# The first MoE's way in by seven block products for two of its three pairs of feature tiles, and one list scheduler for the order of both MoEs

## The chip, the core and the metric

The kernel runs on one core of one Trainium2 chip. Five engines work beside each other, each through its own instructions in order: TensorE (PE) multiplies matrices into PSUM, VectorE (DVE), ScalarE (ACT) and GpSimd (POOL) work on elements, SyncE (SP) issues most DMA transfers. The metric is the device time of one execution, in microseconds (us); lower is better.

## The reference, cut to what matters

```python
mask   = q_bucket[:, :, :, None] == k_bucket[:, :, None, :]      # buckets from 6 sign bits of q @ proj, k @ proj
scores = where(mask, q @ k.T / sqrt(64), -1e9)                   # batch 2, 8 heads, 768 tokens, 64 features
x = softmax(scores) @ v                                          # laid out as 1536 tokens x 512 features
h = maximum(maximum(x @ w1, x @ w2), x @ w3)                     # first MoE: 512 -> 768 ...
x = h @ w_out                                                    # ... -> 512
h = x @ w_in                                                     # second MoE: 512 -> 2048
g = h * (1 / (1 + exp(-1.702 * h)))
out = g @ w_out2                                                 # -> 512
```

The weights are 64-bit floats in memory, everything else is 32-bit.

## The kernel before, in words

Every float32 product is made of three TensorE products: each operand is split into a high part, rounded to the format TensorE takes (`xh`, `whi`), and the low rest (`xl`, `wlo`), and high x high, low x high and high x low are added up in one PSUM bank. A split costs one ACT cast and one subtraction. A matmul of the MoEs multiplies a 128x128 block of weights with 512 tokens; the 1536 tokens make three chunks.

**Attention** fills the first part of the time. Its order is written by a planner (`plan`, with the costs of `COST` and the due times of `DUE`). Its last tasks prepare the first four weight blocks of the first MoE, load two more, and compute chunk 0 of the first feature tile.

**First MoE, way in** (`up1`, L606): six feature tiles of 128, three weight matrices, three chunks: 54 units of 12 matmuls, of which attention's planner issues three. ACT copies a unit of `w1` out of PSUM (L614), DVE takes the maximum with those of `w2` and `w3` (L616), ACT and POOL split the result (L626, L627). **Way out** (`down1`, L639): 12 units of 18 matmuls, split into `xh`, `xl` of the second MoE (L643, L644).

**Second MoE**: eight groups of two feature tiles. The way in of group 0 is dense (`up2`, L667). In groups 1 to 7 the two tiles, with chunks 0 and 1, form a 2x2 block product, which `seven` computes by seven block products of six matmuls in place of eight (L793), from four sums of weight blocks (S1 to S4, made on POOL, L527 to L534, split at L539 and L544) and four sums of tokens (T1 to T4, made once). Chunk 2 stays dense, in half units of six matmuls. P1, P6, P7 and P4 add to one bank one behind another, and ACT copies the bank out between them (L753); P5 and P3 share another, which DVE adds to an earlier copy in between (L749). Then the gelu (L680 to L685), and the **way out** (`down2`, L817), whose result DVE adds to `res` (L822).

**Weight blocks.** A block (128x512, 512 KB as 64-bit words) is loaded into one of two `wraw` buffers (L436) and turned into float32: absolute value on ACT (L450), clamp on POOL (L454), a shift and two bit operations on DVE (L462, L466, L470), then the split, a cast on ACT (L477) and a subtraction on POOL (L497). 58 blocks go through this.

**What sets the order of the MoEs**: `unit` issues a PE unit, then the steps that the unit before left in `due`, then the next step of each weight block in flight (`w_tick`, at a rate of one block per `PACE` units in the first MoE). Every choice of an engine is written in the code. `in_order` then holds each engine to the order of the code. PSUM has eight banks of 128x512 for the MoEs, the weight splits four buffers, `hm` three, `hc` four.

Of the kernel before, what the change touches and what calls it, by code (L numbers as in the profile page):

```python
# [8 lines left out]
U32 = mybir.dt.uint32  # L9
# [80 lines left out]

def build(tc, q, k, v, proj, w1, w2, w3, w_out, m2_in, m2_out, out):
# [23 lines left out]
    shared = ("xh", "xl", "hm0", "wraw", "wbits", "wmag")  # L115
# [292 lines left out]
    for ft in range(FT):  # L408
        for i, w in enumerate((w1, w2, w3)):
            w_block(("up", ft, i), w[:, ft * P:(ft + 1) * P].rearrange("(c p) f -> p c f", p=P), EC, "w")  # L410
    w_out_group(0)
# [6 lines left out]
    for n in range(FT2 // FG):  # L418
        for f in range(n * FG, (n + 1) * FG):
            w_block(("in", f), m2_in[:, f * P:(f + 1) * P].rearrange("(c p) f -> p c f", p=P), EC, "w")  # L420
        if n > 0:
            w_out_group(n)
    WIDE = w1.dtype == U64
    WRAW = 2
    WBUFS = {"w": 4, "wo": 4}
    wraw, wsplit, wf = {}, {}, {}
    wstate = [0, 0]
    wstage = [False]

    def w_load():  # L430
        i = wstate[0]
        if i < len(wblocks):
# [8 lines left out]
            wstate[0] += 1  # L441

    def w_steps(i, fine=False):

        _, n, tag = wblocks[i]
        got = {}

        def magnitude():
            got["m"] = st([P, EC, P], "wbits", 2)[:, :n]
            nc.scalar.activation(got["m"], f32(words()[1]), AF.Abs)  # L450

        def clamp():

            nc.gpsimd.tensor_scalar(out=got["m"], in0=got["m"], scalar1=MOST, scalar2=LEAST, op0=ALU.min, op1=ALU.max)  # L454
# [5 lines left out]
        def shift():  # L460
            got["w"] = st([P, EC, P], "wmag", 4, U32)[:, :n]
            nc.vector.tensor_scalar(out=got["w"], in0=got["m"].bitcast(U32), scalar1=5, scalar2=2, op0=ALU.logical_shift_left,  # L462
                                    op1=ALU.logical_shift_right)

        def low():
            nc.vector.scalar_tensor_tensor(out=got["w"], in0=words()[0], scalar=29, in1=got["w"],  # L466
                                           op0=ALU.logical_shift_right, op1=ALU.bitwise_or)

        def sign():
            nc.vector.scalar_tensor_tensor(out=got["w"], in0=words()[1], scalar=0xC0000000, in1=got["w"],  # L470
                                           op0=ALU.bitwise_and, op1=ALU.bitwise_or)

        def split():
            t = f32(got["w"]) if WIDE else wraw[i][:, :n]
            hi = st([P, EC, P], tag + "hi", WBUFS[tag], F32R, sb if tag == "w" else mo[0])
            lo = st([P, EC, P], tag + "lo", WBUFS[tag], F32R, sb if tag == "w" else mo[0])
            nc.scalar.copy(hi[:, :n], t)  # L477
            got["s"] = (hi, lo, t)
            if not WIDE:
                w_load()  # L480

        def bits():
            shift()
            low()
            sign()
            w_load()

        def whole():
            sign()
            w_load()  # L490
            wf[i] = f32(got["w"])
            if i in wpair:
                wflight.append((None, sum_steps(wpair[i])))

        def lower():
            hi, lo, t = got["s"]
            nc.gpsimd.tensor_tensor(out=lo[:, :n], in0=t, in1=f32(hi[:, :n]), op=ALU.subtract)  # L497
            wsplit[i] = (hi, lo)
        if fine:
            return [magnitude, clamp, shift, low, sign, split, lower]  # L500
        if WIDE and wstage[0]:

            return [magnitude, clamp, None, None, shift, low, whole, None, split, None, lower]
        return ([magnitude, clamp, bits] if WIDE else []) + [split, lower]

    wflight = []

    wpair = {wplace["in", 2 * p + 1]: p for p in range(1, FT2 // 2)}

    def w_free(i):  # L510

        tag = wblocks[i][2]
        mine = [j for j in range(i) if wblocks[j][2] == tag]
        return len(mine) < WBUFS[tag] or mine[-WBUFS[tag]] in wdone

    def sums_free():
        return len(sums) == len(sdone)

    def sum_steps(p):

        a1, a2 = (wf[wplace["in", 2 * p + n]] for n in range(2))
        got = {}

        def first():
            got["x"] = st([P, 2, 2, P], "hm0", 2)
            s1, s2 = (got["x"][:, n] for n in range(2))
            nc.gpsimd.tensor_tensor(out=s1, in0=a2[:, 0:2], in1=a2[:, 2:4], op=ALU.add)  # L527
            nc.gpsimd.tensor_tensor(out=s2, in0=s1, in1=a1[:, 0:2], op=ALU.subtract)

        def second():  # L530
            got["y"] = st([P, 2, 2, P], "hm0", 2)
            s3, s4 = (got["y"][:, n] for n in range(2))
# [20 lines left out]
    def w_tick(start):  # L553

        for entry in list(wflight):
# [4 lines left out]
            if step:  # L560
                step()
# [549 lines left out]
```

## Time and profile before

| what | value |
|---|---|
| median of 3 runs | 695.25 us (694.95 to 695.7) |
| the profiled execution | 695.35 us, span of its trace 693.5 us |
| PE | 687.7 us busy, 99% of the span, 3742 matmuls |
| DVE, ACT, POOL | 73%, 55%, 65% of the span |
| the chain that ended last | PE 92%, DVE 5% |

The span runs from the first to the last instruction of the trace; the execution is 1.85 us longer. The chain that ended last is followed back from the last instruction, at each step to what released it. A share of busy time is a mean over attention and the MoEs, which have different limits.

### The profile page before, as it was taken

Reading aid. Unit: us, or ns where it says so; the run is one execution under the profiler, and the core shown is the slowest. Engines: PE = TensorE matmul, PEld = TensorE weight load, DVE = VectorE, ACT = ScalarE, POOL = GpSimd, SP = SyncE. Lnnn points to the kernel's source line nnn. Section 1 sums busy time; section 2 is a strip of 40 time slices with the busy share of each in tenths; the row PEclk is TensorE's granted clock in tenths of the full one; section 3 lists DMA queues with packets and bytes.
Section 4 is the critical chain, followed back from the end, with each engine's and each line's share of the span. In section 5 each row is a group of like instructions: output and inputs, shape, how many; then the busy total and the mean of one; then the engine's idle time right before and its main releaser. Section 6 shows DMA issues by size and latency. Waiting matters only on the chain.

```text
span 693.5 us, 10887 instructions
## 1 busy us (share of the span) xinstructions
PE 687.7 (99%) x3742; PEld 589.9 (85%) x3742; DVE 503.7 (73%) x888; ACT 379.9 (55%) x745; POOL 452.3 (65%) x492
## 2 busy tenths in 40 slices
PE   9999999999999999999999999999999999999998
PEld 5899999999999988888888888888888888888886
DVE  7999999999999915644554455537878777777855
ACT  4898898888889823323233333565453544444440
POOL 5487878788888845425435432595959678786842
PEclk9999999999999999999999999999999999999999
DMA  5657577778554012322112112013121222212104
GB/s 116 143 126 159 131 176 155 169 170 179 114 125 120 19 39 91 92 64 89 55 60 92 46 53 66 27 60 92 41 81 61 72 67 76 61 60 92 31 0 183
DMA packets 74408, 63.35 MB, mean 91 GB/s; under 512 B 41377, under 2 KB 65185, under 8 KB 74353
## 3 DMA queue, kind: packets, MB, share of 16 engines
q1 hardware_dynamic: 74128, 62.52, 34.7%
q8 instruction: 30, 0.49, 0.3%
q14 instruction: 26, 0.20, 0.1%
q10 hardware_dynamic: 224, 0.13, 0.1%
HBM read 38.80 MB, written 3.15 MB: 60 GB/s over the span
## 4 chain that ended last, share of the span: by engine, by line
PE 92%; DVE 5%; DMA 1%; issue 1%; SPq 0%; ACT 0%; POOL 0%; DVEq 0%; POOLq 0%; ACTq 0%
PE acc L606 20%; PE acc L817 19%; PE acc L793 10%; PE acc L667 8%; PE PV L355 8%; PE S L307 8%; PE T L337 8%; PE acc L639 7%; DVE ptl L347 2%; DVE se L314 2%; PE T L205 2%; PE T L178 1%; PE T L606 1%; DMA raw<-in_v_dram 0%; DMA raw<-in_q_dram 0%
## 5 line engine op out<-in xcount | busy, mean ns | idle before, releaser
L685 POOL TENSOR_TENSOR gl<-hm,gh 128x512 fp32r<-128x512 f32 x48 | 70.1, 1465 | 53.4 <-ACT gh L684 53.4
L328 POOL TENSOR_SCALAR se<-se,rc 128x768 f32<-128x768 f32 x96 | 87.5, 923 | 25.6 <-DVE rc L325 9.1
L347 DVE TENSOR_TENSOR ptl<-T,pth 128x512 fp32r<-128x512 f32 x144 | 94.5, 683 | 4.0 <-ACT pth L343 3.8
L320 ACT ACTIVATE se<-se,mn 128x768 f32<-128x768 f32 x96 | 90.9, 947 | 5.4 <-DVE se L314 4.8
L314 DVE TENSOR_SCALAR_CACHE_REDUCE se<-S 128x768 f32<-128x768 f32 x96 | 91.0, 950 | 1.8 <-PE S L307 1.6
L343 ACT CAST pth<-T 128x512 fp32r<-128x512 f32 x144 | 80.2, 588 | 12.7 <-PE T L337 10.6
L307 PE MATMUL S<-kst,qst 128*128 128x512 f32 (+3 forms) x384 | 87.0, 350 | 0.0
L337 PE MATMUL T<-ident,se 128*128 128x128 f32 x576 | 80.4, 273 | 0.8 <-DVE ptl L347 0.6
L606 PE MATMUL acc<-xh,whi 128*128 128x512 f32 x204 | 79.4, 389 | 0.0
L606 PE MATMUL acc<-xl,whi 128*128 128x512 f32 x204 | 79.4, 389 | 0.0
L606 PE MATMUL acc<-xh,wlo 128*128 128x512 f32 x204 | 79.4, 389 | 0.0
L817 PE MATMUL acc<-wohi,gh 128*128 128x512 f32 (+1 forms) x194 | 75.0, 387 | 0.0
L817 PE MATMUL acc<-wolo,gh 128*128 128x512 f32 (+1 forms) x194 | 75.0, 387 | 0.0
L355 PE MATMUL PV<-pth,vst 128*128 128x256 f32 x288 | 74.4, 293 | 0.0
L462 DVE TENSOR_SCALAR wmag<-wbits 128x512 uint32<-128x512 uint32 (+1 forms) x58 | 43.3, 747 | 38.9 <-POOL wbits L454 38.8
L450 ACT ACTIVATE wbits<-wraw 128x512 f32<-128x512 f32 (+1 forms) x58 | 37.9, 655 | 61.2 <-DMA wraw<-in_moe_w_dram 29.9
L497 POOL TENSOR_TENSOR wlo<-wmag,whi 128x512 fp32r<-128x512 f32 (+1 forms) x42 | 58.9, 1402 | 18.2 <-ACT whi L477 18.2
L337 PEld LDWEIGHTS T<-ident,se 128*128 128x128 f32 x576 | 65.4, 140 | 6.0 <-DVE ptl L347 1.1
L355 PE MATMUL PV<-ptl,vst 128*128 128x256 f32 x288 | 70.2, 279 | 0.0
L616 DVE TENSOR_TENSOR hm<-acc,hm 128x512 f32<-128x512 f32 x34 | 23.5, 690 | 56.8 <-PE acc L606 54.4
L307 PEld LDWEIGHTS S<-kst,qst 76*128 76x128 f32 (+1 forms) x384 | 59.2, 190 | 5.2 <-DVE se L314 0.5
L470 DVE SCALAR_TENSOR_TENSOR wmag<-wraw,wmag 128x512 uint32<-128x512 uint32 (+1 forms) x58 | 61.4, 1058 | 1.4
(163 smaller groups left out, 1604.3 us busy)
## 6 DMA issues: line engine op xcount, KB each, us to landing
wraw<-in_moe_w_dram SPq DMA_DIRECT2D x18, 512.0 KB
wraw<-in_moe_w_out_dram SPq DMA_DIRECT2D x16, 512.0 KB
wraw<-in_moe_w_in_dram SPq DMA_DIRECT2D x16, 512.0 KB
kst<-kq SPq DMA_DIRECT2D x42, 192.0 KB
qst<-kq SPq DMA_DIRECT2D x42, 192.0 KB
raw<-in_k_dram SPq DMA_DIRECT2D x16, 192.0 KB
raw<-in_q_dram SPq DMA_DIRECT2D x16, 192.0 KB
raw<-in_v_dram SPq DMA_DIRECT2D x16, 192.0 KB
```

The lines of the kernel that those rows point to most:

```text
L307: nc.tensor.matmul(pss[:, x], qs[r, k, c * P:(c + 1) * P], ks[r, k, x], start=k == 0, stop=k == 1)
L314: nc.vector.tensor_scalar(out=se[u], in0=pss[:, :S], scalar1=1.0e9, scalar2=None, op0=ALU.min, op1=ALU.min, accum_out=mn[u])
L320: nc.scalar.activation(se[u], se[u], AF.Exp, bias=mn[u], scale=-1.0, accum_out=sm[u // 2][:, u % 2:u % 2 + 1])
L328: nc.gpsimd.tensor_scalar(out=se[u], in0=se[u], scalar1=rc[u // 2][:, u % 2:u % 2 + 1], scalar2=1.0, op0=ALU.mult, op1=ALU.mult)
L337: nc.tensor.transpose(pst[:, i * P:(i + 1) * P], se[2 * jq + o][:, c * P:(c + 1) * P], ident)
L343: nc.scalar.copy(ptr[jq][0][:, n * 512:(n + 1) * 512], tps[jq, n])
L347: nc.vector.tensor_tensor(out=ptr[jq][1][:, s], in0=tps[jq, n], in1=f32(ptr[jq][0][:, s]), op=ALU.subtract)
L355: nc.tensor.matmul(pv[jq], vs[:, c, :], ptr[jq][t].rearrange("p (o c n) -> p c o n", o=2, c=NTILE)[:, c], start=(c == 0 and t == 0), stop= ...
L606: nc.tensor.matmul(o, w[:, c, :], x[:, c, s], start=(c == 0 and z == 0), stop=(c == EC - 1 and z == 2))
L685: nc.gpsimd.tensor_tensor(out=gl, in0=g, in1=f32(gh), op=ALU.subtract)
L793: nc.tensor.matmul(o, w[:, c], x[:, c], start=first and n == 0, stop=n == len(turns) - 1, skip_group_check=True)
L817: nc.tensor.matmul(o, g[:, s], w.rearrange("p c f -> p (c f)")[:, e], start=n == 0, stop=n == len(turns) - 1)
```

## The change

Feature tiles 2 to 5 of the first MoE, in two pairs, take their chunks 0 and 1 by the same seven block products, for each of the three weight matrices: six stages (`STAGES`) of 7 x 6 matmuls and 24 dense ones for chunk 2, in place of 72 matmuls for a pair and a matrix. Tiles 0 and 1 stay dense. For this the sums of weight blocks are made six times more, and the sums of tokens of the first MoE's `x` once (`token_jobs`). The products of a stage follow each other in the order of a string (`t` is a half unit of chunk 2); groups 1 to 7 of the second MoE get a string too.

All work of both MoEs is described as jobs with dependencies and buffers, and `plan_moe`, a list scheduler, writes their order. A job of kind `either` goes to POOL or DVE, whichever the planner thinks ends it first, and the planner holds that a DVE job with SBUF operands and a POOL job exclude each other. `wraw` gets a third buffer, loaded in attention; the absolute value goes straight into `wmag`; blocks of `w_out2` are split only once the way out of the first MoE has been issued.

```diff
...
+def width(kind, n):
+
+    k = n / 960.0
+    return {'copy': [('ACT', .06 + k, False)], 'cast': [('ACT', .09 + k, False)], 'mag': [('ACT', .13 + k, False)],
+            'evac': [('DVE', .16 + k, False)], 'dve': [('DVE', .16 + k, True)], 'shift': [('DVE', .16 + k / 2, True)],
+            'pool': [('POOL', .10 + 2.3 * k, True)], 'clamp': [('POOL', .10 + k, True)],
+            'either': [('POOL', .10 + 2.3 * k, True), ('DVE', .16 + k, True)], 'none': [(None, 0.0, False)],
+            'load': [('SP', 3.0, False)], 'store': [('SP', .1, False)]}[kind]
+
+
...
+def plan_moe(jobs, bufs, begun, free):
...
+    while ready:
+        best = None
+        for n in ready:
+            pick = None
+            for eng, occ, shared in jobs[n][2]:
+                start = max(soon[n], engine.get(eng, 0.0))
+                if shared:
+                    start = max(start, lock['DVE' if eng == 'POOL' else 'POOL'])
+                if pick is None or start + occ < pick[0]:
+                    pick = (start + occ, start, eng, occ, shared)
+            key = (pick[1] + PULL * due[n], n)
+            if best is None or key < best[0]:
+                best = (key, n, pick)
...
+    PLAIN = 2
+    STAGES = [(ft, i) for ft in range(PLAIN, FT, 2) for i in range(3)]
...
-    WRAW = 2
-    WBUFS = {"w": 4, "wo": 4}
+    WRAW = 3
+    BUFS = {"w": 4, "wo": 4, "wmag": 4, "wraw": WRAW, "hm": 3, "hme": 3, "hc": 4, "hm0": 2, "bank": 8, "gs": 6, "sum3": 2, "sum2": 1}
...
+        def whole(name, c, a):
+            def run(eng):
+                s = slice(a * CH, (a + 1) * CH)
+                td[name] = st([P, CH], "hc", 4, pool=mo[0])
+                eng.tensor_tensor(out=td[name], in0=f32(xh[:, c, s]), in1=f32(xl[:, c, s]), op=ALU.add)
+            return run
...
+        for c in range(2):
+            a, b, d, e = ((z, c) for z in "abde")
+            for z, row, col in ((a, c, 0), (b, c, 1), (d, 2 + c, 1), (e, 2 + c, 0)):
+                job(("tok", z), "either", whole(z, row, col), take=[("hc", z)])
+            job(("t", 0, c), "either", less(a, b, a), [("tok", a), ("tok", b)])
+            t_jobs(0, 0, c, a, [("t", 0, c)], 0, [("hc", a)])
+            job(("t", 2, c), "either", less(b, d, b), [("t", 0, c), ("tok", d)])
+            t_jobs(0, 2, c, b, [("t", 2, c)], 0, [("hc", b)])
+            job(("t", 1, c), "either", less(d, d, a), [("t", 2, c), ("t", 0, c)], give=[("hc", a)])
+            t_jobs(0, 1, c, d, [("t", 1, c)], 3, [("hc", d)])
+            job(("t", 3, c), "either", less(e, e, d), [("t", 1, c), ("tok", e)], give=[("hc", d)])
+            t_jobs(0, 3, c, e, [("t", 3, c)], 3, [("hc", e)])
+
...
+    def strassen_jobs(stage, key, tile_, hold, ends, fillers, order, more, place):
...
+        def product(n, weight, token, to, first, deps=(), give=()):
+            def run(eng):
+                o = bank((key, to)) if first else banks[key, to]
+                (wh, wl), (xh, xl) = weights(weight), tokens(token)
+                turns = [(w, x, c) for c in range(2) for w, x in ((wh, xh), (wh, xl))] + [(wl, xh, c) for c in range(2)]
+                for m, (w, x, c) in enumerate(turns):
+                    nc.tensor.matmul(o, w[:, c], x[:, c], start=first and m == 0, stop=m == len(turns) - 1,
+                                     skip_group_check=True)
...
+        def copy(n, to, f, a):
+            def run(eng):
+                held[to] = tile_(f, a)
+                nc.scalar.copy(held[to], banks[key, "x"])
+            job(("c", key, n), "copy", run, [("pe", key, n)], hold(f, a))
+
+        def add(n, to, src, deps, give):
+            def run(eng):
+                nc.vector.tensor_tensor(out=held[to], in0=banks[key, src], in1=held[to], op=ALU.add)
...
+        def p6():
+            product(6, "S2", "T2", "x", False, [("c", key, 1)])
+            copy(6, "u", 0, 1)
+
+        def p7():
+            product(7, "S3", "T3", "x", False, [("c", key, 6)])
+            copy(7, "v", 1, 1)
+
+        def p5():
+            product(5, "S1", "T1", "q", True)
+            add(5, "v", "q", [("pe", key, 5), ("c", key, 7)], False)
+            ends(1, 1, lambda: held["v"], ("a", key, 5), None)
+
+        def p4():
+            product(4, "22", "T4", "x", False, [("c", key, 7)])
+            ends(1, 0, lambda: banks[key, "x"], ("pe", key, 4), ("bank", (key, "x")))
+
+        def p3():
+            product(3, "S4", "22", "q", False, [("a", key, 5)], [("sum" + str(place), key)])
+            add(3, "u", "q", [("pe", key, 3), ("c", key, 6)], True)
+            ends(0, 1, lambda: held["u"], ("a", key, 3), None)
+        made = {"1": p1, "2": p2, "3": p3, "4": p4, "5": p5, "6": p6, "7": p7}
+        fillers = list(fillers)
...
-        one, two = (up2_halves(f + n, NCH - 1) for n in range(FG))
-        return [product("11", "11", "x", True, False, p1), product("12", "21", "w", True, True, p2), one[0],
-                product("S2", "T2", "x", False, False, p6), one[1], two[0],
-                product("S3", "T3", "x", False, False, p7), two[1], product("S1", "T1", "q", True, False, p5),
-                product("22", "T4", "x", False, True, p4), product("S4", "22", "q", False, True, p3)]
...
+        for n, (ft, i) in enumerate(STAGES):
+            stage1_jobs(ft, i, "tt1t6t57243" if n < len(STAGES) - 1 else "12t65t7t43t")
+        key = ("up", *STAGES[-1])
+        job(("late",), "none", switch(["sb_t"], "sb_h2", 3), [("~", "pe", key, n) for n in range(1, 8)])
...
+                stage2_jobs(p, "tt1t6t57243")
...
-        task("raw", NU - 8, w_load, deps=[("w", AHEAD - 2, 4)], cost="wraw")
-        task("raw", NU - 8, w_load, deps=[("w", AHEAD - 1, 4)], cost="wraw")
+        for n in range(AHEAD - WRAW, AHEAD):
+            task("raw", NU - 8, w_load, deps=[("w", n, 4)], cost="wraw")
...
-        for a in range(1, NCH):
-            for i in range(3):
-                unit(up1, 0, i, a, bank, after=(lambda: split1(0, a)) if i == 2 else None)
-        for ft in range(1, FT):
-            for i in range(3):
-                for a in range(NCH):
-                    unit(up1, ft, i, a, bank, after=(lambda: split1(ft, a)) if i == 2 else None)
...
```

**PE, group 4 of the second MoE: from the end of P7 to P4.** `acc` is a bank, `th`, `tl` a token sum, `shi`, `slo` a weight sum. Before, behind P7: half a dense unit (L667), P5 (on `acc_6745`), then P4, which adds to P7's bank:

```order
L667 MATMUL acc_6710<-xh_5149,whi_6544 128x512
L667 MATMUL acc_6710<-xl_5150,whi_6544 128x512
L667 MATMUL acc_6710<-xh_5149,wlo_6545 128x512
L667 MATMUL acc_6710<-xh_5149,whi_6544 128x512
L667 MATMUL acc_6710<-xl_5150,whi_6544 128x512
L667 MATMUL acc_6710<-xh_5149,wlo_6545 128x512
L793 MATMUL acc_6745<-th_1172_5221,shi_6579 128x512
L793 MATMUL acc_6745<-tl_1173_5222,shi_6579 128x512
L793 MATMUL acc_6745<-th_1172_5221,shi_6579 128x512
L793 MATMUL acc_6745<-tl_1173_5222,shi_6579 128x512
L793 MATMUL acc_6745<-th_1172_5221,slo_6580 128x512 x2
L793 MATMUL acc_6649<-th_1231_5570,whi_6544 128x512
```

Now, from P7's last row on: P2 (on `acc_6811`), then P4 on P7's bank `acc_6733`:

```order
L850 MATMUL acc_6733<-th_1211_5445,slo_6710 128x512 x2
L850 MATMUL acc_6811<-xh_5244,whi_6649 128x512
L850 MATMUL acc_6811<-xl_5245,whi_6649 128x512
L850 MATMUL acc_6811<-xh_5244,whi_6649 128x512
L850 MATMUL acc_6811<-xl_5245,whi_6649 128x512
L850 MATMUL acc_6811<-xh_5244,wlo_6650 128x512 x2
L850 MATMUL acc_6733<-th_1241_5649,whi_6689 128x512
```

Two products stood between P7 and P4, with twelve matmuls; now it is one, with six. The stages of the first MoE have the same order.

**DVE, the way out of group 3 of the second MoE.** `res` is the result, `wmag` a weight block, `hm_1466` and `hm_1468` a weight sum. Before:

```order
L822 TENSOR_TENSOR res_5662<-acc_6562,res_5662 128x512
L822 TENSOR_TENSOR res_5681<-acc_6571,res_5681 128x512
L462 TENSOR_SCALAR wmag_6583<-wbits_6534 128x512
L822 TENSOR_TENSOR res_5696<-acc_6585,res_5696 128x512
L466 SCALAR_TENSOR_TENSOR wmag_6583<-wraw_6450,wmag_6583 128x512
L822 TENSOR_TENSOR res_5707<-acc_6596,res_5707 128x512
L470 SCALAR_TENSOR_TENSOR wmag_6583<-wraw_6450,wmag_6583 128x512
L822 TENSOR_TENSOR res_5720<-acc_6610,res_5720 128x512
L822 TENSOR_TENSOR res_5729<-acc_6618,res_5729 128x512
L822 TENSOR_TENSOR res_5742<-acc_6629,res_5742 128x512
L462 TENSOR_SCALAR wmag_6637<-wbits_6594 128x512
L822 TENSOR_TENSOR res_5754<-acc_6639,res_5754 128x512
```

Now:

```order
L1098 TENSOR_TENSOR res_5777<-acc_6621,res_5777 128x512
L599 TENSOR_TENSOR wlo_6650<-wmag_6449,whi_6649 128x512
L579 TENSOR_SCALAR wmag_6524<-wmag_6524 128x512
L1098 TENSOR_TENSOR res_5791<-acc_6632,res_5791 128x512
L584 SCALAR_TENSOR_TENSOR wmag_6524<-wraw_6471,wmag_6524 128x512
L1098 TENSOR_TENSOR res_5803<-acc_6641,res_5803 128x512
L589 SCALAR_TENSOR_TENSOR wmag_6524<-wraw_6471,wmag_6524 128x512
L754 TENSOR_TENSOR hm_1466_6692<-wmag_6524 128x256
L758 TENSOR_TENSOR hm_1468_6696<-wmag_6449,wmag_6524 128x256
L599 TENSOR_TENSOR wlo_6690<-wmag_6524,whi_6689 128x512
L756 TENSOR_TENSOR hm_1466_6692<-hm_1466_6692,wmag_6449 128x256
L760 TENSOR_TENSOR hm_1468_6696<-wmag_6449,hm_1466_6692 128x256
```

The weight sums (128x256) and the subtraction for `wlo` moved from POOL to DVE, and a few rows on those for `slo` and the gelu's `gl`.

**SP, late in attention.** `xm` is a part of the attention's result, `kst`, `qst` the stacked operands of a head's scores. Before:

```order
L381 DMA xm_3197<-xt_3196 64x256
L436 DMA wraw_3226<-in_moe_w_dram 128x4x256
L381 DMA xm_3283<-xt_3282 64x256
L226 DMA kst_3341<-kq_3170 64x768
L226 DMA kst_3341<-kq_3171 64x768
```

Now:

```order
L487 DMA xm_3194<-xt_3193 64x256
L550 DMA wraw_3223<-in_moe_w_dram 128x4x256
L487 DMA xm_3280<-xt_3279 64x256
L550 DMA wraw_3303<-in_moe_w_dram 128x4x256
L332 DMA kst_3340<-kq_3167 64x768
L332 DMA kst_3340<-kq_3168 64x768
L332 DMA qst_3341<-kq_3200 64x768 x2
```

One more weight load stands ahead of the transfers of a head's operands. On the other engines the order of attention is as before.

## Rows read from the trace of the kernel before

**Rows 1.** the page's part 1: busy time, share of the span, instructions of each engine

```profile
PE 687.7 (99%) x3742; PEld 589.9 (85%) x3742; DVE 503.7 (73%) x888; ACT 379.9 (55%) x745; POOL 452.3 (65%) x492
```

**Rows 2.** the chain that ended last in order of time: start us, us, what

```profile
210.69 0.70 PE S L307 x4
250.83 138.72 PE acc L606 x612
389.55 48.96 PE acc L639 x216
541.97 1.36 PE acc L793 x6
543.33 1.36 PE acc L667 x6
544.69 4.08 PE acc L793 x18
673.98 16.45 PE acc L817 x78
```

**Rows 3.** busy us (instructions) of PE, PEld, DVE, ACT, POOL; clock, DMA share, GB/s

```profile
251.00:389.50 138.50, 138.50 (x613) 114.68 (x612) 69.38 (x94) 42.57 (x75) 61.33 (x57) 1.00 0.23 71
517.50:548.80 31.30, 31.30 (x139) 25.90 (x138) 23.83 (x33) 14.11 (x26) 23.62 (x21) 1.00 0.22 68
```

**Rows 4.** by line and form, 251 to 389.5: busy us, mean ns | idle before

```profile
L497 POOL TENSOR_TENSOR wlo<-wmag,whi 128x512 fp32r<-128x512 f32 x14 | 18.6, 1330 | 5.1 <-ACT whi L477 5.1
L454 POOL TENSOR_SCALAR wbits<-wbits 128x512 f32<-128x512 f32 x16 | 11.8, 738 | 20.3 <-ACT wbits L450 20.3
L614 ACT COPY hm<-acc 128x512 f32<-128x512 f32 x17 | 9.6, 580 | 4.1 <-PE acc L606 4.1
```

**Rows 5.** DVE in order of time: start us, us, engine, line, op [idle before <-releaser]

```profile
518.09 0.68 DVE L683 TENSOR_TENSOR hm<-acc,hm 128x512 f32<-128x512 f32 x1
518.68 0.68 DVE L683 TENSOR_TENSOR hm<-hc,hm 128x512 f32<-128x512 f32 x1
519.28 0.69 DVE L466 SCALAR_TENSOR_TENSOR wmag<-wraw,wmag 128x512 uint32<-128x512 uint32 x1
519.88 0.68 DVE L822 TENSOR_TENSOR res<-acc,res 128x512 f32<-128x512 f32 x1
520.49 1.19 DVE L470 SCALAR_TENSOR_TENSOR wmag<-wraw,wmag 128x512 uint32<-128x512 uint32 x1
540.25 0.42 DVE L462 TENSOR_SCALAR wmag<-wbits 128x512 uint32<-128x512 uint32 x1
546.15 0.69 DVE L749 TENSOR_TENSOR hc<-acc,hc 128x512 f32<-128x512 f32 x1 [1.41 <-PE acc L793]
```

**Rows 6.** POOL in order of time, beside the DVE rows above

```profile
519.50 3.33 POOL L685 TENSOR_TENSOR gl<-hm,gh 128x512 fp32r<-128x512 f32 x2 [1.35 <-ACT gh L684]
```

**Rows 7.** ACT in order of time, behind a product of the second MoE

```profile
543.47 0.57 ACT L753 COPY hc<-acc 128x512 f32<-128x512 f32 x1
```

**Rows 8.** by line and form, 471 to 690

```profile
L454 POOL TENSOR_SCALAR wbits<-wbits 128x512 f32<-128x512 f32 x24 | 14.8, 617 | 4.5 <-ACT wbits L450 4.5
```

**Rows 9.** all engines in order of time, at the first MoE's start

```profile
249.14 0.74 POOL L394 TENSOR_TENSOR xl<-xf,xh 128x256 fp32r<-128x256 f32 x1
250.67 0.39 PE L606 MATMUL acc<-xh,whi 128*128 128x512 f32 x1
```

**Rows 10.** SP's queue in order of time, late in attention

```profile
192.47 0.59 SPq L436 DMA_DIRECT2D wraw<-in_moe_w_dram  x1
197.79 1.19 SPq L226 DMA_DIRECT2D kst<-kq  x2
```

**Rows 11.** stretches late in attention, columns as in group 3

```profile
193.00:196.00 3.00, 3.00 (x23) 2.73 (x22) 3.00 (x7) 2.99 (x7) 2.82 (x4) 1.00 0.66 199
198.00:206.00 8.00, 8.00 (x62) 7.61 (x63) 7.97 (x18) 6.22 (x15) 7.37 (x9) 1.00 0.82 175
206.00:210.00 4.00, 3.62 (x30) 3.28 (x30) 3.96 (x11) 4.00 (x10) 3.49 (x6) 1.00 0.17 44
```

More of the change, by code (lines that the diff above doesn't have):

```diff
@@ L469, in sign @@
[L469 to L480, printed above, removed]
@@ L501, in w_steps @@
[L501 to L517, printed above, removed]
@@ L586, in build @@
+        return [magnitude, clamp, shift, low, sign, split, lower]
+    def w_get(*key):
+        return wsplit[wplace[key]]
     NTOK = B * S
     NCH = NTOK // CH
[L588 to L609 removed]
+    jobs = []
@@ new lines, in build, with job, pe @@
+    engines = {"POOL": nc.gpsimd, "DVE": nc.vector, "ACT": nc.scalar, "PE": nc.tensor, "SP": nc.sync, None: None}
+    last_pe = [None]
+    def job(name, kind, fn, deps=(), take=(), give=(), n=CH):
+        jobs.append((name, fn, width(kind, n), list(deps), list(take), list(give)))
+    def pe(name, count, fn, deps=(), take=(), give=()):
+        deps = list(deps) + ([("~", *last_pe[0])] if last_pe[0] else [])
+        occ = count * .2275
+        jobs.append((name, fn, [('PE', occ, False)], deps, list(take), list(give)))
+        last_pe[0] = name
@@ new lines, in w_jobs, with step @@
+    def w_jobs(i, extra=()):
+        src, n, tag = wblocks[i]
+        if i >= AHEAD + WRAW:
+            job(("ld", i), "load", lambda eng: w_load(), take=[("wraw", i)])
+        size = n * P
+        held = {}
+        def step(m):
+            def run(eng):
+                if not held:
+                    held.update(enumerate(w_steps(i)))
+                held[m](eng)
+            return run
+        row = [("mag", "mag", [("ld", i)], [("wmag", i)], []), ("clamp", "clamp", [], [], []), ("shift", "shift", [], [], []),
+               ("low", "dve", [], [], []), ("sign", "dve", [], [], [("wraw", i)]),
+               ("split", "cast", list(extra), [(tag, i)], []), ("lower", "either", [], [], [("wmag", i)])]
+        for m, (name, kind, deps, take, give) in enumerate(row):
+            deps = deps + ([(row[m - 1][0], i)] if m else [])
+            job((name, i), kind, step(m), deps, take, give, size)
@@ new lines, in t_jobs, with high, low @@
+    def t_jobs(stage, n, c, z, deps, place, give):
+        def high(eng):
+            if (stage, n) not in ts:
+                ts[stage, n] = tuple(st([P, 2, CH], f"t{s}{n}", 1, F32R, mo[place]) for s in "hl")
+            nc.scalar.copy(ts[stage, n][0][:, c], td[z])
+        def low(eng):
+            eng.tensor_tensor(out=ts[stage, n][1][:, c], in0=td[z], in1=f32(ts[stage, n][0][:, c]), op=ALU.subtract)
+        job(("th", stage, n, c), "cast", high, deps)
+        job(("tl", stage, n, c), "either", low, [("th", stage, n, c)], give=give)
@@ L804, in down2, with down2_jobs @@
+    def down2_jobs(p, t, last, ends):
         a, j = divmod(t, CH // P)
         s = slice(j * P, (j + 1) * P)
[L806 to L807 removed]
         b, c = divmod(t, NTILE)
```

807 lines of the change are left out of this document (486 added, 321 removed).

## The prediction

> **What bounds the kernel now.** I read the page's busy shares first, then the chain of waits, then the busy times by stretch, and last the engines in order of time. PE is busy for 99% of the span [rows 1]. The chain says more: from 250.83 us on it is PE alone, one unit behind the other: 612 matmuls of the first MoE's way in take 138.72 us and 216 of the way out 48.96 us, without a piece of another engine between them; the second MoE runs on in the same way, its last piece the 78 matmuls from 673.98 us on [rows 2]. 138.72 / 612 = 0.2267 us for a matmul of 512 columns; a half unit or a block product of six takes 1.36 us [rows 2], the same rate. The clock is granted in full (1.00, the 2.4 GHz level) [rows 3]. So in the MoEs the time is the number of matmuls times 0.2267 us, as long as DVE, ACT, POOL and the loads keep ahead of PE; and there they are at half load: DVE 69.4, ACT 42.6 and POOL 61.3 us of 138.5 in the first way in [rows 3].
>
> **What the change removes.** A stage (pair of feature tiles, one weight matrix) has 7 x 6 + 24 = 66 matmuls in place of 72; there are six stages, so 36 matmuls go, all in a stretch where PE waits for nothing: 36 x 0.2267 = 8.16 us. The profiled execution took 695.35 us (693.5 of span and 1.85 around it); without them 687.19 us. The median of the runs shown is 0.10 us lower, so either base gives the same to a tenth.
>
> **What it adds, on DVE.** Counted in the new order between the first and the last matmul of the way in (51 units before, and what replaces them): DVE has 177 operations in place of 93, POOL 29 in place of 57, ACT 97 in place of 74. What does a DVE operation cost? Records of 128x512 are 0.68 to 0.69 us long, but the next one starts 0.60 us after: 518.09, 518.68, 519.28, 519.88, 520.49, through operands in PSUM, in SBUF and the bit operations alike [rows 5]. So 136 wide operations (8 of them on 384 columns, taken as 512) cost 136 x 0.60 = 81.6 us, 17 shifts at 0.42 [rows 5] 7.1. A two-operand DVE operation of 128x256, of which there are 24, is not in the trace: it lies between half of 0.60 and 0.60, so 7.2 to 14.4 us together; I take 0.35, nearer the half, since the length follows the columns: 8.4. Sum 97.1 us (95.9 to 103.1). POOL: 16 clamps at 0.738 and 13 subtractions at 1.330 [rows 4], 29.1 us. PE's stretch is 138.72 - 8.16 = 130.56 us. DVE fills 74% of it, and even if no DVE and POOL operation ever ran at once, 97.1 + 29.1 = 126.2 us fit. ACT's 97 at 0.58 [rows 4] are 56 us. So the work fits; its cover is PE's own stretch, and where the cover is thin is shown next.
>
> The planner counts 0.693 us for a wide DVE operation (0.16 + 512/960, in `width`); its order was laid for a slower DVE than rows 5 show. That speaks for DVE running early, not late.
>
> **DVE in the second MoE.** Its matmuls stay, but POOL's subtractions and sums move to DVE. A group lasts 138 matmuls, 31.28 us; before, DVE was busy 23.8 us of it and POOL 23.6 [rows 3]. Now DVE has 41 wide operations, 4 shifts and 4 half ones: 24.6 + 1.7 + 1.4 = 27.7 us; POOL keeps 4 clamps at 0.617 [rows 8], 2.5 us. That is 89%, serially 30.2 us: it fits, with 1.1 us to spare. This is the thinnest of the load balances, and it comes seven times.
>
> One rule of the Trainium skill speaks against the change here. What the trace shows is the step of 0.60 us between starts of records of 0.68 [rows 5]. The Trainium skill (VectorE: DVE Perf Modes, "The DRAIN you can't avoid") says that the next Vector operation does not start until the pipe of the one before is empty. Taken as one whole record behind another it would be 0.68 per operation and the slower rival below; the trace does not agree, since each starts 0.08 to 0.09 us before the record ahead has ended.
>
> **Waits that get shorter cover.** P1, P6, P7 and P4 add to one bank, and ACT must copy it between them. Before, 12 matmuls (2.72 us) stood between two of them; now six (1.36 us) stand between P1 and P6 and between P7 and P4. In the trace P7 runs from 541.97 to 543.33 [rows 2], the copy from 543.47 to 544.04 [rows 7]: 0.71 us from the product's end. So 0.65 us are left, about one ACT operation (0.58) that is under way when the copy is due. Behind the copy stands PE with the next product, and all of PE's queue behind it. There are 13 stages with two such places, less one for the last stage of the first MoE: 25. Bounds: nothing at each (ACT free or one operation ahead), and 0.5 us at each if two stand ahead, 12.5 us in all. I take 0.2 us for all of them, near the lower bound: the same distance is already in the trace between P5 and P3 (P4 stands between): the product's end at 546.05, 1.36 us into the piece from 544.69 [rows 2], DVE's addition from 546.15 to 546.84 [rows 5], P3 at 547.41; 0.57 us were left, with an operation of 0.69, and PE did not wait in any of seven groups.
>
> **First stage.** It needs the token sums and the first weight sums. PE gets there after 15 dense units (40.8 us), two half units, P1 and a half unit: 46.2 us behind 250.67 [rows 9]. Up to the last subtraction for S2, DVE has 26 us of work in the new order and POOL 14: nothing, with 6 us left even in series. **Way out.** The high and low parts of tiles 4 and 5 take the room of the token sums and can only be written when P3 of the last stage has read them. PE then has 6 + 13 matmuls (4.3 us) before it reads the low part of tile 4; a cast and a subtraction take 0.58 + 0.68 and two handovers of 0.1. Nothing. **Chunk 2** of feature tile 0 now comes second instead of after three units, and its last part of `xl` is read 5.0 us after 250.67; POOL ended it at 249.88 [rows 9]. Nothing.
>
> **The load in attention.** The third `wraw` buffer puts a 512 KB load in front of the operands of a head, which SP issues from 197.79 us on [rows 10]. A load issued at 192.47 [rows 10] kept the DMA engines 66% busy for 3 us, 2.0 us of all of them; the head's operands had them 82% busy from 198 to 206 and little after [rows 11]. So they land about 0.5 + 2.0 us later, near 208.6, and the first scores of that head are computed at 210.69 [rows 2]. Nothing; if that cover were gone, at most the 2.5 us.
>
> **Sum:** 695.35 - 8.16 + 0.2 = 687.4 us.
>
> **Rivals.** (a) *The copies block PE.* ACT holds its queue in order, and casts that wait for DVE stand in front of some copies. At 0.1 to 0.25 us per place, 2.5 to 6.2 us come back: 689.9 to 693.4 us. For it: 0.65 us is little. Against: ACT's load is 45%. If it took 0.33 us each, the gain would be gone. (b) *A single late stage*: the first token sums, the head's operands, or the hand-over to the way out, 1 to 4 us: 688.4 to 691.4 us. For it: these are new chains; against: the margins above. (c) *Slower: DVE becomes the bound of the second MoE.* At 0.68 per wide operation and 0.4 per half one a group has 27.9 + 1.7 + 1.6 = 31.2 us on DVE, with the clamps in series 33.7, 2.4 us more than PE's 31.28; seven groups give 16.8 us back, 704 us. It decides from 1.17 us per group on (8.16 / 7). For it: 520.49 took 1.19 us [rows 5] beside POOL's two, 3.33 us instead of 2 x 1.33 [rows 4, 6], so DVE and POOL do hold each other up; against: after the change POOL has hardly anything left to hold DVE up with. (d) *The count of matmuls does not set the time*, and 36 fewer change nothing: 695 us. Against it is the equal rate in every piece of rows 2.
>
> **Chances.** The forecast, 686.6 to 688.4 us: 0.70. (a) 0.11, (b) 0.08, (c) 0.07, (d) 0.04. The range reaches into (a) and (b), 686.4 to 691.5 us, and leaves out (c), (d) and the far end of (a), the 0.5 us per place with it. What this kernel's measurement can tell from no change is 0.2%, 1.4 us: faster than that are the forecast, (b) and nearly all of (a), 0.89; the same 0.04; slower 0.07.
>
> **What would show it.** Right: PE's chain through both MoEs without another engine, 3706 matmuls, the way in 130.6 us long, the rest as before, DVE near 28 us per group of the second MoE with steps of 0.60 us. Wrong: waits of PE for an ACT copy before P6 or P4 (a); one gap at the first T product, at the head's scores or at the way out (b); groups of the second MoE longer than 31.3 us with DVE busy throughout (c).

## The result, and the profile of the changed kernel

The changed kernel takes 686.68 us (686.52 to 686.98, 4 runs), the kernel before 695.1 us (694.86 to 695.7, 4 runs). The ratio is 0.9878, with a 95% interval of 0.9861 to 0.9895: 8.4 us or 1.2% faster, where 687.4 us was forecast and 8.16 us of the difference was put down to 36 matmuls. The profiled execution took 686.98 us, 685.2 of them span.

Part 1 of the page of the changed kernel (columns as in [rows 1]):

```profile
PE 679.7 (99%) x3706; PEld 583.7 (85%) x3706; DVE 591.8 (86%) x1099; ACT 400.6 (58%) x777; POOL 284.6 (42%) x359
```

PE has 36 matmuls and 8.0 us less. DVE has 88 us more and POOL 168 us less, and neither shows in the time. Where PE's 8 us went is seen in the chain of the changed kernel:

```profile
210.69 0.70 PE S L413 x4
...
250.85 43.52 PE acc L661 x192
294.37 1.36 PE acc L850 x6
...
381.41 48.96 PE acc L956 x216
...
533.73 6.80 PE acc L850 x30
...
665.65 16.40 PE acc L1090 x78
682.07 0.42 DVE res L1098
```

Set this beside [rows 2]. The scores of the head whose operands load late start at 210.69 in both. The way in starts at 250.85 (250.83 before) and ends at 381.41 (389.55): 130.56 us in place of 138.72, the forecast to the hundredth. The way out takes 48.96 us in both; the last piece starts 8.33 us earlier. So all but 0.2 us of the 8.33 lies in the one stretch from which matmuls were taken.

All waits of PE in the span of the changed kernel (engine, line, waited for: us, times, longest):

```profile
PE S L248 <- DVE warm L245: 1.3, 1, 1.3
PE T L443 <- DVE ptl L453: 0.6, 2, 0.3
PE T L284 <- DVE ptl L453: 0.2, 1, 0.2
```

All are in attention or ahead of it. In both MoEs PE waits for nobody, neither at the 25 places with the shorter cover nor at the three new chains that were priced at zero. The busy times by stretch (columns as in [rows 3]) show how much room there was:

```profile
198.00:206.00 8.00, 8.00 (x62) 7.62 (x63) 7.97 (x18) 6.24 (x15) 7.32 (x9) 1.00 0.92 222
206.00:210.00 4.00, 3.65 (x31) 3.33 (x30) 3.96 (x11) 4.00 (x10) 3.49 (x6) 1.00 0.35 93
251.00:381.30 130.30, 130.30 (x577) 107.92 (x576) 114.20 (x180) 55.28 (x98) 33.58 (x33) 1.00 0.20 63
508.50:539.80 31.30, 31.30 (x140) 25.93 (x139) 27.14 (x47) 13.95 (x26) 3.01 (x4) 1.00 0.16 52
```

The first two are the load that was moved in front of a head's operands: the DMA share rises from 0.82 to 0.92 and behind it from 0.17 to 0.35 [rows 11], and PE's 210.69 does not move. A group of the second MoE (last row) has DVE busy 27.1 us and POOL 3.0, forecast 27.7 and 2.5. In the way in, DVE's records fill 114.2 us, 17 more than the 97.1 forecast by steps. That is not the counting, since time in which two records overlap is counted once: 23 of the 180 records are longer than their usual 0.69 or 0.42 us, by 14.9 us together, and each of the 23 stands beside a POOL record. It is still less than PE's 130.3.

What an operation costs without POOL beside it (DVE in order of time):

```profile
520.13 0.42 DVE L754 TENSOR_TENSOR hm<-wmag 128x256 f32<-128x256 f32 x1
520.47 0.42 DVE L758 TENSOR_TENSOR hm<-wmag,wmag 128x256 f32<-128x256 f32 x1
520.81 0.69 DVE L599 TENSOR_TENSOR wlo<-wmag,whi 128x512 fp32r<-128x512 f32 x1
521.41 0.42 DVE L756 TENSOR_TENSOR hm<-hm,wmag 128x256 f32<-128x256 f32 x1
```

The operation of 128x256 that the trace of before did not have starts 0.34 us ahead of the next (520.13, 520.47, 520.81) with a record of 0.42; 0.35 was taken, between 0.30 and 0.60. The wide one behind it has a step of 0.60, as in [rows 5].

Two of the copies with the shorter cover, on ACT:

```profile
529.68 0.59 ACT L867 COPY hc<-acc 128x512 f32<-128x512 f32 x1 [0.26 <-PE acc L850]
...
536.48 0.59 ACT L867 COPY hc<-acc 128x512 f32<-128x512 f32 x1 [0.73 <-PE acc L850]
```

ACT stood idle for 0.26 and 0.73 us until the product had ended, so nothing was ahead of the copy. The second belongs to P7, the second of the five products of 1.36 us in the chain's piece from 533.73: P7 ends at 536.45, the copy 0.62 us later at 537.07, and P4 starts at about 537.81: 0.74 us to spare.

### The profile page after: what moved, and what is told of

Its sections match the earlier page's. It is cut to its first block, busy times and chain, and to the rows that moved or that the text cites. A ratio compares the mean times of both kernels' runs of the same rounds, so it can differ in the third digit from the quotient of the medians.

```text
span 685.2 us, 10869 instructions
## 1 busy us (share of the span) xinstructions
PE 679.7 (99%) x3706; PEld 583.7 (85%) x3706; DVE 591.8 (86%) x1099; ACT 400.6 (58%) x777; POOL 284.6 (42%) x359
## 4 chain that ended last, share of the span: by engine, by line
PE 95%; DVE 2%; DMA 1%; issue 0%; ACT 0%; SPq 0%; ACTq 0%; DVEq 0%
PE acc L1090 19%; PE acc L661 19%; PE acc L850 18%; PE S L413 9%; PE PV L461 9%; PE T L443 8%; PE acc L956 7%; PE T L311 2%; PE T L284 1%; PE T L661 1%; DVE ptl L453 1%; DVE se L420 1%; PE S L248 1%; PE T L352 0%; DMA raw<-in_v_dram 0%; DMA raw<-in_q_dram 0%
## 5 line engine op out<-in xcount | busy, mean ns | idle before, releaser
L575 POOL TENSOR_SCALAR wmag<-wmag 128x512 f32<-128x512 f32 (+1 forms) x58 | 44.8, 776 | 219.8 <-ACT wmag L568 206.0
L661 PE MATMUL acc<-xh,whi 128*128 128x512 f32 x188 | 73.1, 389 | 0.0
L661 PE MATMUL acc<-xl,whi 128*128 128x512 f32 x188 | 73.1, 389 | 0.0
L661 PE MATMUL acc<-xh,wlo 128*128 128x512 f32 x188 | 73.1, 389 | 0.0
L1098 DVE TENSOR_TENSOR res<-acc,res 128x512 f32<-128x512 f32 (+1 forms) x85 | 56.4, 677 | 7.2 <-PE acc L1090 6.9
L1090 PE MATMUL acc<-wohi,gl 128*128 128x512 f32 (+1 forms) x194 | 59.3, 387 | 0.0
L461 PEld LDWEIGHTS PV<-pth,vst 128*128 128x128 f32 x288 | 54.3, 189 | 1.1
L461 PEld LDWEIGHTS PV<-ptl,vst 128*128 128x128 f32 x288 | 54.4, 189 | 0.0
L594 ACT CAST whi<-wmag 128x512 fp32r<-128x512 f32 (+1 forms) x42 | 25.2, 603 | 46.5 <-DVE wmag L589 31.9
```

The lines of the kernel that those rows point to most:

```text
L461: nc.tensor.matmul(pv[jq], vs[:, c, :], ptr[jq][t].rearrange("p (o c n) -> p c o n", o=2, c=NTILE)[:, c], start=(c == 0 and t == 0), stop= ...
L661: nc.tensor.matmul(o, wz[:, c, :], xz[:, c, s], start=first and c == cs[0] and z == 0, stop=last and c == cs[-1] and z == 2)
L1090: nc.tensor.matmul(o, g[:, s], w.rearrange("p c f -> p (c f)")[:, e], start=n == 0, stop=n == len(turns) - 1)
L1098: nc.vector.tensor_tensor(out=res[t][:, e], in0=o, in1=res[t][:, e], op=ALU.add)
```

## The experiments

Three questions: is it the number of matmuls that makes the gain (theory A), or do the planner's orders and the third buffer have a part in it (B); what does the copies' cover cost (a); how near is DVE to its limit (C). Ratios are to the kernel before on the same chip, each with its 95% interval.

**The changed kernel again.**

> The changed kernel once more, to be compared with the other variants on the same chip. Both theories: 686.7 us, a ratio to the kernel before of 0.988 (8.16 us less for 36 matmuls at 0.2267 us).

686.99 us (686.64 to 687.27), before 695.49; 0.9877 (0.9862 to 0.9892). This is the base for the four runs that follow.

**All pairs dense, the rest of the change kept.**

```diff
-    PLAIN = 2
+    PLAIN = 6
-        token_jobs()
-        for n, (ft, i) in enumerate(STAGES):
-            stage1_jobs(ft, i, ...)
```

> All three pairs of the first MoE's way in dense (3742 matmuls, the count of before); the planner's choice of engines, its orders for the second MoE and the third weight buffer stay. Theory A (in the MoEs the time is the number of matmuls times 0.2267 us, the rest of the change is worth nothing): 695.1 us, the time of before, within 0.5 us. Rival B (a part of the gain comes from the new orders, the engines or the buffer): clearly between 686.7 and 695.1, for example 693 if a quarter of it does.

695.58 us (10 runs), before 695.49; 1.0001 (0.9992 to 1.0011). With every product dense, the planner, its choice of engines and the third buffer are worth nothing: B has fallen. The piece of its chain for the first MoE's way in, and the busy times there:

```profile
251.42 138.72 PE acc L661 x612
```

```profile
251.40:390.00 138.60, 138.60 (x614) 114.74 (x613) 78.75 (x127) 40.62 (x70) 13.30 (x21) 1.00 0.22 69
```

POOL's 61.3 us of [rows 3] have become 13.3, DVE's 69.4 have become 78.8, and PE's 138.72 are the same to the hundredth.

**One pair by seven products.**

```diff
-    PLAIN = 2
+    PLAIN = 4
```

> One pair of the first MoE's way in by seven products in place of two (3724 matmuls, 18 fewer than before and 18 more than after). Theory A: half of the 8.16 us, 695.1 - 4.1 = 691.0 us, within 0.4. Rival E (a cost paid once, for the token sums or the late stage, lies under the gain): one pair then gains less than half, 691.5 us or more.

692.25 us (691.59 to 692.5); 0.9951 (0.9937 to 0.9966). That is 1.25 us above what A gave; 0.4 of it is the base, since the kernel before took 695.49 us beside this run and not 695.1. By the time alone rival E would still have it. The trace says otherwise:

```profile
251.20 92.48 PE acc L661 x408
...
385.84 48.96 PE acc L956 x216
```

The way in lasts 385.84 - 251.20 = 134.64 us, 4.08 us less than 138.72, half of the gain exactly. The rest of the surplus lies outside: attention ended 0.37 us later than in the trace of before, and the time around the span was 1.8 to 2.9 us in these four runs (1.8 to 2.3 in those of the kernel before). Why the latter varies no run shows.

**No cover for the first copy of a stage.**

```diff
-            stage1_jobs(ft, i, "tt1t6t57243" if ...)
+            stage1_jobs(ft, i, "tttt1657243" if ...)
-                stage2_jobs(p, "tt1t6t57243")
+                stage2_jobs(p, "tttt1657243")
```

> Order of the products within a stage changed so that P6 comes right after P1, which adds to the same bank, with nothing in between: PE must wait there until ACT has copied the bank, in 12 stages (5 of the first MoE, 7 of the second). Count of matmuls as after (3706). Theory A with the copy's price from rows 7 (0.71 us from a product's end to the copy's end, 0.1 us on top for PE to start): 12 x 0.75 = 9 us more than after, 695.7 us, and the whole gain is gone; the waits stand in the chain as ACT's copies. Rival (PE has enough other work queued behind, or the copy is not in its way): 687 us.

699.09 us (698.66 to 699.39), before 695.24; 1.0054 (1.0039 to 1.0069): 12.1 us more than after, one microsecond for each of the 12 places, and slower than before the change. Its chain at one place, without the pieces between P1 and P6, and the same place on PE and ACT in order of time:

```profile
538.44 1.37 PE acc L850 x6
...
540.47 8.46 PE acc L850 x36
```

```profile
539.83 0.58 ACT L867 COPY hc<-acc 128x512 f32<-128x512 f32 x1 [0.70 <-PE acc L850]
540.47 0.50 PE L850 MATMUL acc<-th,shi 128*128 128x512 f32 x1 [0.68 <-ACT hc L867]
540.81 0.39 PE L850 MATMUL acc<-tl,shi 128*128 128x512 f32 x1
```

The wait is 0.68 us (0.73 at two of the twelve places), near the 0.71 of [rows 7]. The other 0.3 us comes behind it, at PE's restart: the matmul behind the wait is followed after 0.34 us and not after 0.23, and the 36 matmuls from there take 8.46 to 8.48 us in its chain, not 8.16. A wait of PE costs more than its row says.

**The long cover of before.**

```diff
-            stage1_jobs(ft, i, "tt1t6t57243" if ...)
+            stage1_jobs(ft, i, "12t6tt7t543" if ...)
-                stage2_jobs(p, "tt1t6t57243")
+                stage2_jobs(p, "12t6tt7t543")
```

> The order of the seven products with the long cover of before (12 matmuls, 2.72 us, between any two products of one bank), for all stages but the last of the first MoE; all else as after. Theory A (1.36 us of cover was enough, the copies cost nothing): 686.9 us, no difference from after beyond 0.4 us. Rival (a) (part of the gain is lost to the copies at 25 places): faster than after by 0.5 us or more.

686.97 us (686.76 to 687.54); 0.9881 (0.9866 to 0.9896). The same as after. (Its long cover is that of the bank which ACT copies; between P5 and P3, on the other bank, six matmuls stand, as before the change.) Six matmuls of cover, 1.36 us, are as good as twelve, and no cover at all costs 1 us a place: rival (a) has fallen, and the 0.2 us that the forecast allowed for it is not seen.

**The moves to DVE undone.**

```diff
-            'either': [('POOL', .10 + 2.3 * k, True), ('DVE', .16 + k, True)], ...
+            'either': [('POOL', .10 + 2.3 * k, True)], ...
```

> Subtractions and sums that the planner may put on DVE or POOL go to POOL alone. Counted load: way in of the first MoE DVE 55 and POOL 113 of 130.6 us; a group of the second MoE DVE 19 and POOL 21.5 of 31.3 us. Matmuls as after (3706). Theory A (any engine may do it as long as it keeps ahead of PE): the second MoE stays at 31.3 us a group; in the first way in POOL at 87% is close to its limit, since its operations take 1.56 us and not 1.33 when DVE runs beside it (113 becomes up to 130): 687 to 690 us. Rival (the move to DVE was needed for the second MoE too, POOL's latency of 1.33 us breaks the chains): groups longer than 31.3 us, 695 us or more.

697.53 us (696.84 to 698.27), before 695.24; 1.0031 (1.002 to 1.0043). The rival had the time, but not for its reason, and theory A had neither: the 36 matmuls are gone, and the kernel is slower than before. By stretch:

```profile
251.00:393.50 142.50, 136.86 (x587) 108.47 (x585) 78.78 (x101) 55.62 (x97) 115.72 (x107) 1.00 0.18 55
504.20:535.50 31.30, 31.30 (x140) 25.93 (x139) 21.87 (x33) 14.53 (x26) 21.41 (x21) 1.00 0.21 68
...
289.50:306.60 17.10, 14.11 (x60) 10.75 (x59) 1.43 (x3) 5.77 (x10) 17.10 (x17) 1.00 0.06 23
```

The second MoE runs at 31.28 us a group with POOL busy 21.4: there the move to DVE was not needed, and my rival fell. The loss lies in the first MoE. Its way in and its way out, from 250.83 to 440.35 in the chain below, take 189.52 us in place of 179.52 (250.85 to 430.37 in after): 10.0 us more, although POOL is busy for only 115.7 of the 142.5 in the first row, which ends at a wait behind eleven matmuls of the way out. The third row shows why a sum over the stretch was the wrong measure. From 289.5 to 306.6 POOL has not a free moment while DVE has 1.4 us of work, and it came there with a backlog: from 262 to 306.6 it is busy for 43.1 of 44.6 us. The chain there:

```profile
250.83 35.38 PE acc L661 x156
...
292.93 2.51 POOL hl L690 x2
295.44 1.24 POOL slo L773
296.69 3.74 POOL tl L793 x3
300.42 1.24 POOL hc L805
...
440.35 16.32 PE acc L661 x72
```

POOL works off the low parts of finished tiles, of a weight sum and of the token sums, and the next token sum, one after the other, and PE stands behind them. The two largest waits of PE in this kernel's MoEs (us, times, longest):

```profile
PE acc L850 <- ACT hm L867: 1.9, 1, 1.9
PE acc L850 <- POOL tl L793: 1.4, 3, 0.9
```

PE stands still nine times in the first MoE, 5.7 us together; six of these waits, 4.5 us, lie between 298 and 313.5 us. With 0.3 us for each restart that is 8.4 of the 10.0 us; among the rest are weight loads of PE that came late without a standstill (six matmuls take 1.56 and 1.49 us at 364.50 and 366.06). No run tried another order of POOL's work, so the loss is that of this planner's order.

**Two raw weight buffers.**

```diff
-    WRAW = 3
+    WRAW = 2
```

> Two raw weight buffers of 512 KB in place of three, as before the change; all else as after (3706 matmuls). Theory A (the loads are far enough ahead with two): 686.9 us within 0.4, and the extra load in attention is gone. Rival (the seven products take their weights in quicker bursts and the third buffer carries them): waits of ACT and DVE on weight loads that reach PE, 688 us or more.

687.38 us (686.81 to 687.73); 0.9883 (0.9866 to 0.9899). That is 0.4 us above after, no difference that can be told. In its profile the first MoE starts at 251.49, 0.64 us later than in after's, and each piece of the chain from there is as long as in after's: the third buffer does not carry the gain.

**More work for DVE.**

```diff
                     nc.vector.tensor_tensor(out=res[t][:, e], in0=o, in1=res[t][:, e], op=ALU.add)
+                    if p < 7 and t % 2 == 0:
+                        x = res[(t + 1) % 12]
+                        nc.vector.tensor_tensor(out=x, in0=x, in1=x, op=ALU.max)
```

> After every second addition of a way-out tile in groups 1 to 6 of the second MoE, DVE does one more operation of 128x512 that changes nothing (the maximum of a result tile and itself): 6 more per group, 6 x 0.60 = 3.6 us. A group of after has DVE busy 27.1 us of 31.3, so 30.7 us of work by busy time: still under PE's 31.28. Theory A (free as long as DVE keeps ahead of PE): no change, 686.9 us within 0.5. Rival C (with so little to spare DVE's queue delays PE already at 98%): PE waits for DVE in the chain, 1 us a group or more, 693 us.

687.69 us (687.36 to 688.22), before 695.53; 0.9889 (0.9873 to 0.9906). A group of it:

```profile
539.80:571.10 31.30, 31.30 (x140) 25.93 (x139) 30.92 (x55) 14.33 (x25) 3.48 (x4) 1.00 0.21 68
```

DVE's records fill 30.9 of 31.3 us, 99%, and PE stands still nowhere in either MoE: six more operations a group cost next to nothing. The chain shows one late product, in the last group, behind the added operations of the one before:

```profile
658.72 6.99 PE acc L850 x30
```

That is 0.19 us over the usual 6.80: P4 started late behind an ACT copy, and the cast ahead of this copy had waited for DVE. From the first MoE's start to the last DVE operation it is 431.44 us (250.70 to 682.14) against 431.22 in after (250.85 to 682.07), 0.2 us more. The time is 0.7 us above the repeat of after, just beyond the half microsecond allowed; the rest of it lies outside the MoEs, and the intervals overlap.

The same after every addition, not every second:

> The same after every addition in groups 1 to 6: 12 more operations, 12 x 0.60 = 7.2 us a group; 27.1 + 7.2 = 34.3 us of DVE by busy time (33.2 by steps of 0.60) against PE's 31.28. Both theories: DVE is the bound of these groups, each is 2 to 3 us longer, 6 x 2.0 to 6 x 3.0: 699 to 705 us, and PE waits for DVE in the chain. If the time stayed at 687 us, DVE's step would be much shorter than the records say.

712.01 us (710.52 to 712.88); 1.0234 (1.0219 to 1.0249). DVE does become the bound, as rival (c) had it, but at 25 us and not 12 to 18: its chain runs mainly through DVE from 502 to 686 us, and PE's waits for ACT's copies (L867) stand behind it. PE's waits in the second MoE:

```profile
PE acc L850 <- ACT hc L867: 13.5, 11, 2.9
PE acc L850 <- DVE hc L872: 4.0, 3, 2.5
```

They make 17.5 us in 14 places. Behind twelve of them a restart costs 0.3 us, 3.6 us in all; behind the other two the clock fell, as in this stretch:

```profile
505.00:507.00 2.00, 0.37 (x2) 0.33 (x3) 1.73 (x3) 2.00 (x5) 0.00 (x0) 0.99 0.26 39
507.00:509.00 2.00, 2.00 (x6) 1.60 (x5) 1.21 (x2) 1.26 (x3) 0.61 (x1) 0.50 0.61 223
509.00:511.00 2.00, 2.00 (x7) 1.53 (x6) 0.87 (x2) 0.92 (x2) 0.00 (x0) 0.65 0.00 0
```

Behind its standstill PE gets a granted clock of 0.50, its level of 1.2 GHz, then 0.65 and from 511 us on 1.00 again. The chain has twelve matmuls there:

```profile
506.63 4.63 PE acc L850 x12
...
686.86 4.61 PE acc L850 x12
```

4.63 us in place of 2.72, and once more in the last group, 4.61: two times 1.9 us, with the restart in it. 17.5 + 3.6 + 3.8 = 24.9 us against 25.0 measured.

The two standstills were 2.03 and 2.85 us long. But the one between them in length left the clock at 1.00 (PE, and the stretch behind it):

```profile
617.24 0.50 PE L850 MATMUL acc<-xh,shi 128*128 128x512 f32 x1 [2.49 <-DVE hc L872]
```

```profile
618.00:620.00 2.00, 2.00 (x10) 1.64 (x10) 1.84 (x4) 1.52 (x3) 0.00 (x0) 1.00 0.00 0
```

So the length of one standstill does not decide it; what does, these runs do not show.

**A faster version: the first group of the second MoE by seven products as well.**

```diff
-        seven.update((("in", 2 * p + 1), ("in", 2 * p)) for p in range(1, FT2 // FG))
+        seven.update((("in", 2 * p + 1), ("in", 2 * p)) for p in range(FT2 // FG))
-        for n in range(NCH * FG):
-            up2_jobs(n % FG, n // FG)[0]()
-            if p:
-                stage2_jobs(p, "tt1t6t57243")
-            order = range(tiles) if p == 0 else [(t + 2 * CH // P) % tiles for t in range(tiles)]
+            stage2_jobs(p, "tt1t6t57243" if p else "12tt56t7t43")
+            order = [(t + 2 * CH // P) % tiles for t in range(tiles)]
```

> The second MoE's first group (dense in both kernels) by seven products too: 3700 matmuls, 6 fewer than after. Theory A: 1.36 us less than after, 685.3 us, PE without a wait in the MoEs. Rival C (other engines are near their limit): DVE's work for the way out of the first MoE, the new token sums and this group's weight sums meets on 50 us; PE then waits at the group's first products and the time is 686.7 us or more.

686.3 us (686.11 to 686.87); 0.9866 (0.985 to 0.9883). It is 0.7 us below the repeat of after, and the intervals overlap. The way in and the later groups are those of after; the way out into the new group lost 0.47 us of the 1.36, since PE came to the first way-out products before their operands were ready (one weight load of PE stood 0.39 us for ACT's line 1023, another 0.36 us for DVE's line 1026).

The same with the order of the other groups:

> The second MoE's first group by seven products as in group0, but with the order of the other groups (tt1t6t57243), in place of one that ended on the additions for all tiles. 3700 matmuls. Theory A: the wait of 0.4 us before the second way-out product that group0 showed goes, and the time is 1.36 us below after: 685.6 us, the second MoE eight equal groups of 31.28 us. Rival C (the sums for the first group come too late for P6): PE waits before the group's second product, and the time is no better than group0's.

686.28 us (686.03 to 686.51), before 695.53; 0.9866 (0.9852 to 0.9881). The wait moved and did not go: it stands ahead of P6, the group's second product and the first with a token sum, where rival C had put it. But it is not the sums that come late. The chain runs through ACT, which must copy P1's bank first (L867):

```profile
431.26 1.56 ACT th L790 x3
...
435.17 0.60 ACT hm L1016
435.77 0.48 ACT hc L867
...
436.30 1.67 PE acc L850 x6
```

```profile
433.88 1.28 ACT L1016 ACT_TABLE_LOAD   x1
```

ACT has casts, copies and activations of the old and the new stage in one queue there, and ahead of the first activation of the gelu a table load of 1.28 us. From the first MoE's start to the last DVE operation the two versions take 430.34 and 430.42 us against 431.22 in after, so 0.9 and 0.8 us of the 1.36 are there in the traces. By the time both lie 0.7 us or 0.1% below after, with runs from 686.03 to 686.87 against 686.64 to 687.27: less than the 0.2% that this measurement can tell from no change.

## Why the prediction was right

- **What bounds the kernel, and the sum.** 36 matmuls at 0.2267 us came out as 8.16 us in the one stretch where they had been; half of them gave 4.08 us in the same stretch, and with none taken the time was that of before (1.0001). Rival (d) has fallen with that.
- **DVE's cost.** Steps of 0.60 us and 0.34 us for the half operation are right, and 27.1 us a group of the second MoE against 27.7. In the way in the term was too small: 97.1 us by steps stand against 114.2, since the sum had no term for the records that POOL lengthens (14.9 us); POOL was busy for 33.6 us, not 29.1. The prediction knew this hold-up from [rows 5] and [rows 6], used it for rival (c) alone, and was saved by the room left: its bound without any overlap, 126.2 us, was not passed. The sentence of the Trainium skill that was weighed (VectorE: DVE Perf Modes, "The DRAIN you can't avoid") would have given 0.68 a step if one whole record stood behind another. The same section adds that an operation which is not held starts earlier, which the prediction left out; with its steps of 0.60 the trace after agrees with that.
- **The cover of the copies.** The copy's 0.71 us and the 0.65 us left were close, 0.62 and 0.74 us at the P4 shown, and pricing them near nothing was right: PE waited at none of the 25 places and the longer cover gained nothing. The term of 0.2 us measured zero. What was too small is the price without any cover, expected ahead of that run at 0.75 us a place: it is 1.0, since the restart took 0.3 us and not 0.1.
- **The zeros.** The first stage, the way out, chunk 2 and the load in attention had no wait, as forecast. For the load, DMA did run 0.92 busy to 206 us and still 0.35 to 210 us, and the scores began at 210.69 all the same.
- **Rival (c), the thin balance on DVE.** It was placed right, and the balance had more room than "1.1 us to spare" in series: six operations more a group cost 0.2 us in all. Past the limit the price expected, 2 to 3 us a group, was too low, because a waiting PE also pays restarts and clock.
- **A reason that did not carry.** The text found that the work fits because the loads add up to less than PE's stretch. For DVE that held up to 99%. For POOL it did not: at 115.7 us of 142.5 it cost 10.0 us, most of it where its work for the first stage came due. The move to DVE, priced only as a cost, is what lets the 36 matmuls count in the orders tried: with POOL alone the planner's order makes the kernel slower (1.0031).

## What to carry to other kernels

Where PE is the chain without a break, count its matmuls, and then ask of every other engine not whether its load fits into the stretch but whether what comes due at one place fits into the time ahead of that place. A cover of one product was enough, and without any cover each place cost a microsecond: look for the point where the cover is gone, not for the longest cover. And price a wait of PE at its length plus 0.3 us, and where it stands for microseconds also with the clock behind it.

## What the runs showed of the hardware

- After two standstills of PE, of 2.03 and 2.85 us, the granted clock was 0.50 in the next full stretch of 2 us and 0.65 to 0.68 in the one behind it, and twelve matmuls took 4.6 us in place of 2.72; after one of 2.49 us in the same kernel, and after waits of 0.7 us (the kernel without cover), it stayed at 1.00.
- DVE and POOL hold each other up, but not where DVE's operation reads PSUM. In the trace of before, from 251 us on, 51 of the 72 DVE records of 128x512 that stand beside POOL with operands in SBUF alone are longer than 0.72 us; of the 123 beside POOL with an operand in PSUM none is, and none of the 103 without POOL (shifts left out). POOL's side is the same: in the kernel with POOL alone, its subtractions of 128x512 have records of 1.27 to 1.32 us where DVE is idle (32 of them) or only reads PSUM beside them (39), and up to 1.79 us, 1.45 in the mean, beside DVE operations in SBUF alone (35). Three POOL subtractions of the changed kernel with two of the DVE operations beside them, one in SBUF alone and one that reads PSUM (`acc`):

```profile
279.33 4.61 POOL L793 TENSOR_TENSOR tl<-hc,th 128x512 fp32r<-128x512 f32 x3
```

```profile
279.57 1.77 DVE L810 TENSOR_TENSOR hc<-hc,hc 128x512 f32<-128x512 f32 x1
281.27 0.68 DVE L701 TENSOR_TENSOR hm<-acc,hm 128x512 f32<-128x512 f32 x1
```

  The move to DVE leaves little of this, since POOL has few operations left.
- ACT too starts the next operation before the record ahead has ended: in the chain of the last version three casts take 1.56 us, 0.52 each, with records of 0.62 elsewhere.
